# Sliding-window attention with a gated SwiGLU branch on one core: scores in sixteen 32x32 tiles, first loads in smaller pieces

## The chip, the core and the metric

The kernel runs on one core of a Trainium2 chip. A core has TensorE (PE, matrix multiplies, with its weight loads shown apart as PEld), VectorE (DVE), ScalarE (ACT), GpSimd (POOL) and SyncE (SP, which here only issues DMAs). The metric is the device time of one execution in microseconds; smaller is better.

## The reference

For one sequence of 2048 tokens of width 512, the output mixes two branches by a gate per token. Branch a is attention with 32 heads of 16 dimensions, where a query sees its own token and the 255 before it; branch b is a SwiGLU feed-forward network of inner width 1376.

```python
g = sigmoid((x * gate_w).sum(-1, keepdims=True))
qkv = (x @ wqkv).reshape(B, S, 3, H, Dh)          # H = 32, Dh = 16, W = 256
scores = einsum("bhqd,bhkd->bhqk", q, k) * Dh ** -0.5
mask = (i_q - i_k >= 0) & (i_q - i_k < W)
p = softmax(where(mask, scores, -1e9))
a = einsum("bhqk,bhkd->bhqd", p, v).reshape(B, S, D) @ wo
b = (silu(x @ w1) * (x @ w3)) @ w2
return g * a + (1 - g) * b
```

## The kernel before

Everything is in bf16 with f32 sums. The sequence is cut into four chunks t of 512 tokens, and the 32 heads into four groups c of eight heads (128 rows of Q and K).

**Attention.** `add_proj` (line 294) projects K and Q of a group and a chunk. K is written twice, with the even heads' rows zeroed in one copy and the odd heads' in the other (`maskEO`), so that 32 rows hold two heads and 128 columns hold 64 keys for the even head and the same 64 keys for the odd one. A score step, called a burst (`add_burst`, line 664), takes two or three pieces: each is a block of 64 keys with the queries of this chunk that can see any of them, up to 320. `bursts` (line 272) lists the pieces; their columns add up to 512 at most. For each piece four matmuls with 32 rows and 128 columns of weights (line 685) write the scores of eight heads, transposed, into four PSUM banks called `big`. There is one `big`, so a burst waits until the previous burst's exp has read it. ACT takes the exp of the whole of it (line 693) into an `e` tile; triangles at the near and far end of each piece are then zeroed by POOL (affine_select, line 709) or DVE (a minimum with `keep`, line 703). There are 76 bursts, 19 for each group. The product with V (`add_pv`, line 730; matmuls at line 759) takes the `e` tiles of a chunk in eight tiles of 64 rows and 32 columns, with a column of ones in V for the denominators; DVE transposes, divides and transposes back into `OT`.

**Feed-forward, gate and output.** `add_up` (line 442) makes gate and up products and their swish, `add_up_last` the last 96 inner rows in tiles of 128x32 (line 505), `add_down` (line 543) the second product; `add_out` (line 574) multiplies by `wo`, mixes and stores, in two DMAs a row block for m under 8 and in one for the rest. `add_last` does the last row block.

**Order.** The kernel plans itself: each piece of work is an `Op` with engines, a duration and what it waits for; a list scheduler (lines 873 to 1003) places them by these costs, and the instructions are then issued in that order, engine by engine. Bursts have due times, `T0 + PACE * n`. Once placed, an engine's order is fixed, and the chip's engines meet through semaphores alone.

**Start.** TensorE runs six warm-up matmuls on a zeroed tile (line 1008). Meanwhile the first loads are issued: SP issues x0 and x1 (256 tokens each), q0 (both of the first two groups' Q weights), k1, v, and then transposing loads and feed-forward weights; ACT issues k0. The first 512 tokens are transposed by TensorE (`add_tx`, line 230), which needs the identity `ident` from POOL, and copied to `xT` by DVE and ACT; later tokens come through transposing DMAs.

Of the kernel before, what the change touches and what calls it, by code (L numbers as in the profile page):

```python
# [8 lines left out]
ACT = mybir.ActivationFunctionType  # L9
# [5 lines left out]
WIN = 256  # L15
P = 128
# [6 lines left out]
def kernel(  # L23
# [77 lines left out]
    def slot(pool, key):  # L101
        return slot_of[(pool, key)]

    warm = sb.tile([P, 1, P], BF16, name="tt0")
    nc.vector.memset(warm[:], 0.0)
    nc.vector.memset(scr[:], 0.0)  # L106
    xs_tiles = {}

    def x_dma(t, h):
        xs = xp.tile([P, 2, D], BF16, name=f"xs{h}")[:]  # L110
        nc.sync.dma_start(
            out=xs,
            in_=x2d[512 * t + 256 * h:512 * t + 256 * (h + 1), :].rearrange("(m p) d -> p m d", p=P))
        xs_tiles[2 * t + h] = xs

    def xt_dma(t, c):
        nc.sync.dma_start_transpose(out=xT[:, c, 512 * t:512 * (t + 1)],
# [13 lines left out]
        land[name] = at  # L131

    nc.scalar.activation(out=scr[:, 1:2], in_=scr[:, 0:1], func=ACT.Tanh)
    dma("x0", "SP", 3.8, lambda: x_dma(0, 0))
    dma("x1", "SP", 4.8, lambda: x_dma(0, 1))
    dma("k0", "ACT", 4.6, lambda: w_dma(nc.scalar, wk_sb, A_wqkv, 0, P, D))
    dma("q0", "SP", 6.2, lambda: w_dma(nc.sync, wq_sb, A_wqkv, 0, 2 * P))
    dma("k1", "SP", 7.0, lambda: w_dma(nc.sync, wk_sb, A_wqkv, P, 2 * P, D))
    dma("v", "SP", 8.5, lambda: w_dma(nc.sync, wv_sb, A_wqkv, 0, D, 2 * D))
    dma("x2", "SP", 11.2, lambda: [xt_dma(1, c) for c in range(NDC)])  # L140
    FA = 4 * P
    dma("wa", "SP", 14.4, lambda: (w_dma(nc.sync, w1_sb, B_w1, 0, FA),
# [87 lines left out]
    def add_tx(m2):  # L230

        xT_op[m2] = []
        for half in range(2):
            key = ("tx", m2, half)
            hold("g", key, 1)
            cs = slice(2 * half, 2 * half + 2)

            def pe(key=key, half=half):
                tx = bank(key, BF16, (P, 2, 2, P))
                for j in range(2):  # L240
                    for c in range(2):
                        d0 = (2 * half + c) * P
                        nc.tensor.transpose(out=tx[:, j, c, :], in_=xs_tiles[m2][:, j, d0:d0 + P],
                                            identity=ident[:])

            def evac(eng, key=key, cs=cs):
                dst = xT[:, cs, 2 * m2 * P:(2 * m2 + 2) * P].rearrange("p c (j t) -> p j c t", j=2)
                if eng == "ACT":
                    nc.scalar.copy(out=dst, in_=g_tile[key][:])
                else:  # L250
                    nc.vector.tensor_copy(out=dst, in_=g_tile[key][:])

            a = Op("PE", 0.25 if m2 > 1 else 0.43, pe, [loads[f"x{m2}"]], acq=[("g", key)], kind="tx")
            a.first, a.need = m2 < 2, 9.0
            xT_op[m2].append(Op("ACT" if half else "DVE", 0.55 if half else 0.36, evac, [a],
                                rel=[("g", key)], rank=-1))

    def xdep(t0, t1):

        r = []  # L260
        for c in range(NDC):
            r.append([xT_op[m2][c // 2] if m2 < 2 else loads["x2" if m2 < 4 else "x4" if m2 < 6 else "x6"]
                      for m2 in range(t0 // 256, (t1 + 255) // 256)])
        return r

    LAST = (NDC - 1, NTC - 1)
# [27 lines left out]
    def add_proj(c, t0, t1, is_q):  # L294


        key = ("q" if is_q else "k", c, t0)
        t = t0 // 512
        hold("g", key, 1)
        n = t1 - t0  # L300
        o0 = t0 - 512 * t
        first = (c, t, "alloc") not in qk_tile
        if first:
            hold("qk", (c, t), len(bursts(c, t)) + (len(bursts(c, t + 1)) if t + 1 < NTC else 0))

        def pe(d0):
            def fn():
                if (c, t) not in qk_tile:
                    i = slot("qk", (c, t))
                    qk_tile[(c, t)] = (sb.tile([P, 1024], BF16, name=f"kt{i}"),  # L310
                                       sb.tile([P, 512], BF16, name=f"qt{i}"))
                b = bank(key) if d0 == 0 else g_tile[key]
                for dc in range(d0, d0 + 1):
                    nc.tensor.matmul(b[:, 0:n], lhsT=(wq_sb if is_q else wk_sb)[:, dc, c * P:(c + 1) * P],  # L314
                                     rhs=xT[:, dc, t0:t1], start=(dc == 0), stop=(dc == NDC - 1))
            return fn

        def evac_q(eng):
            qt = qk_tile[(c, t)][1]
            if eng == "ACT":  # L320
                nc.scalar.copy(out=qt[:, o0:o0 + n], in_=g_tile[key][:, 0:n])
            else:
                nc.vector.tensor_copy(out=qt[:, o0:o0 + n], in_=g_tile[key][:, 0:n])

        def evac_k(eng):
            kt = qk_tile[(c, t)][0][:, 2 * o0:2 * (o0 + n)].rearrange("p (j i b) -> p j i b", i=2, b=HK)
            src = g_tile[key][:, 0:n].rearrange("p (j x b) -> p j x b", x=1, b=HK)
            sh = [P, n // HK, 2, HK]
            nc.vector.tensor_tensor(out=kt, in0=src.to_broadcast(sh), in1=maskEO[:].to_broadcast(sh),
                                    op=ALU.mult)  # L330

        w = loads[("q0" if is_q else f"k{c}") if c <= 1 else "kq"]
        a0, a = pe_unit(0.216 * NDC * n / 512, [pe(i) for i in range(NDC)],
                        [w] + ([] if first else [qk_tile[(c, t, "alloc")]]),
                        acq=[("g", key)] + ([("qk", (c, t))] if first else []), kind="proj",
                        more=xdep(t0, t1))
        if first:
            qk_tile[(c, t, "alloc")] = a0
        d = 0.68 * n / 512 + 0.03
        if is_q:  # L340
            bs = [Op(("ACT", "DVE"), d, evac_q, [a], rel=[("g", key)], rank=-0.5)]
            Q_op.setdefault(c, []).append((t0, t1, bs))
        else:
            bs = [Op("DVE", 1.16 * n / 512 + 0.05, evac_k, [a], rel=[("g", key)], rank=-0.5)]
            K_op.setdefault(c, []).append((t0, t1, bs))
        return a0
# [227 lines left out]
    def add_out(m, n0=0, n1=512):  # L574
# [13 lines left out]
        def fin(eng):  # L588
            ot = smpool.tile([P, D], BF16, name="ot")
            nc.vector.scalar_tensor_tensor(out=ot[:, 0:n], in0=g_tile[key][:, 0:n],  # L590
                                           scalar=gq[:, m:m + 1], in1=bsb[:, m, n0:n1],
                                           op0=ALU.mult, op1=ALU.add)
            for i in range(0, n, n // (2 if m < 8 else 1)):
                j = i + n // (2 if m < 8 else 1)
                nc.sync.dma_start(out=out2d[m * P:(m + 1) * P, n0 + i:n0 + j], in_=ot[:, i:j])

        a0, a = pe_unit(0.87 * n / 512, [pe(i) for i in range(NDC)], [pv_out[(c, m)] for c in range(NDC)] + [loads["wo"], down_pe[m]],
# [66 lines left out]
    def add_burst(c, t, n):  # L664


        key = (c, t, n)
        pieces = bursts(c, t)[n]
        w = sum(q1 - q0 for _, q0, q1, _ in pieces)
# [3 lines left out]
        for j, q0, q1, _ in pieces:  # L673
            deps += cover(K_op, c, HK * j, HK * j + HK) + cover(Q_op, c, q0, q1)
        deps = list(dict.fromkeys(deps))
        tl = {}

        def pe():
            qt = qk_tile[(c, t)][1]
            big = ps.tile([P, 4, 512], F32, name="big")  # L680
            tl["big"] = big
            for j, q0, q1, col in pieces:
                kt = qk_tile[(c, j // 8)][0]
                for u in range(4):
                    nc.tensor.matmul(big[:, u, col:col + q1 - q0],  # L685
                                     lhsT=kt[32 * u:32 * u + 32, (j % 8) * P:(j % 8 + 1) * P],
                                     rhs=qt[32 * u:32 * u + 32, q0 - 512 * t:q1 - 512 * t],
                                     start=True, stop=True)

        def ex(eng):  # L690
            e = sb.tile([P, 4, 512], BF16, name=f"e{slot('e', key)}")
            e_tile[key] = e
            nc.scalar.activation(out=e[:, :, 0:w], in_=tl["big"][:, :, 0:w], func=ACT.Exp,  # L693
                                 scale=SCALE)

        def mask(cols, far):
            def f(eng):
# [14 lines left out]
                                                channel_multiplier=1 if far else -1)  # L712
            return f

        a = Op("PE", 0.21 + 0.22 * w / 512, pe, deps, acq=[("big", key)], kind="burst",
               rel=[("qk", (c, t))] + ([("qk", (c, t - 1))] if t else []))
        b = Op("ACT", 0.13 + 1.75 * w / 512, ex, [a], rel=[("big", key)], acq=[("e", key)],
               rank=-1, kind="exp")
# [82 lines left out]
            pv_out[(c, m)] = o  # L801
        return a

    T0, PACE, NWARM = 11.5, 2.59, 6
    SEQ = [(t, n) for t in range(NTC) for n in range(len(bursts(0, t)))]
    per_c = len(SEQ)

# [13 lines left out]
    for c in range(NDC):  # L821
        pieces = [(0, 256), (256, 512)] if c == 0 else [(0, 512)]
        pieces += [(512 * t, 512 * t + 512) for t in range(1, NTC)]
        for t0, t1 in pieces:
            for is_q in ((True, False) if (c, t0) == (1, 0) else (False, True)):
                a = add_proj(c, t0, t1, is_q)
                lead = (4.0 if is_q or t0 else 5.0) if c == 0 else 6.0 + (4 - t0 / 512) * 4.0
                a.need = when(c, first_use(c, t0, t1, is_q)) - lead
# [176 lines left out]
    with tc.manual_schedule():  # L1005
        b = ps.tile([P, 512], F32, name="g0")
        for i in range(NWARM):
            nc.tensor.matmul(b[:], lhsT=warm[:, 0, :], rhs=warm[:].to_broadcast([P, 4, P]), start=(i == 0),  # L1008
                             stop=(i == NWARM - 1))
        done = set()  # L1010
        for o in order:
            if not wo_t and o in burst_ops[7:] and done.issuperset(z_op[0:4]):
# [34 lines left out]
```

The softmax here doesn't subtract the row's maximum and nothing guards it: scores larger than these inputs give would overflow.

## Time and profile before

| what | value |
|---|---|
| median of 3 runs | 231.02 us (231.02 to 231.4) |
| the profiled execution | 230.87 us |
| its span, first to last instruction | 229.2 us |
| granted TensorE clock over the span | 1.0 |
| weight loads and matmuls | 3060 each |
| matmuls of the bursts (line 685) | 720 in 76 bursts |
| matmuls of the V product (line 759) | 1440 in 16 runs |
| x0 / x1 landed | 3.93 / 5.02 us |

"Busy" of an engine is the time in which at least one of its instructions ran. Matmuls are pipelined: a record runs from the start of a matmul to its modelled end, which comes well after the next one has started, so starts are what to compare. "Idle before" is the time in which an engine ran nothing before a group, with what ended it.

### The profile page before, as it was taken

How to read it: one execution, taken by the hardware profiler on the slowest of the kernel's cores; microseconds unless marked ns; L12 is line 12 of the kernel's file. 1: busy time of each engine (PE TensorE's matmuls, PEld its weight loads, DVE VectorE, ACT ScalarE, POOL GpSimd, SP SyncE). 2: the span in 40 equal slices, each digit the busy share in tenths (PEclk: the TensorE clock that was granted, in tenths of full speed). 3: DMA queues.
4: the chain of work that ended last, by engine and by line, in shares of the span. 5: the costliest groups of instructions: out<-in, count | busy, mean ns of one | idle time of the engine just before them, and what ended most of it. 6: DMA issues, size and time to landing. Idle time of an engine off the chain costs nothing.

```text
span 229.2 us, 7274 instructions
## 1 busy us (share of the span) xinstructions
PE 224.8 (98%) x3060; PEld 101.2 (44%) x3060; DVE 180.9 (79%) x316; ACT 175.5 (77%) x144; POOL 174.7 (76%) x395
## 2 busy tenths in 40 slices
PE   7999999999999999999999999999999999999995
PEld 3544434544344443544353435444443444354544
DVE  1688599999998997879758596959987688876754
ACT  3578889788989989787989897987899877977030
POOL 8058888888899898888878887877888878777200
PEclk9999999999999999999999999999999999999999
DMA  6999999401000000000000000000000001220202
GB/s 186 235 255 301 234 268 338 112 0 27 26 3 3 3 0 0 3 4 4 0 3 0 3 3 3 0 3 4 0 3 1 3 4 37 70 82 0 94 3 93
DMA packets 20081, 13.81 MB, mean 60 GB/s; under 512 B 8656, under 2 KB 19760, under 8 KB 20048
## 3 DMA queue, kind: packets, MB, share of 16 engines
q1 hardware_dynamic: 18944, 11.93, 18.8%
q0 software_dynamic: 432, 1.25, 2.8%
q8 instruction: 24, 0.39, 0.7%
q10 hardware_dynamic: 672, 0.16, 0.3%
q14 instruction: 9, 0.07, 0.1%
HBM read 8.55 MB, written 2.10 MB: 46 GB/s over the span
## 4 chain that ended last, share of the span: by engine, by line
PE 97%; DMA 2%; SPq 0%; DVE 0%; issue 0%
PE big L685 11%; DMA xs_93<-in_A_x_dram 2%; PE g_1928 L553 1%; PE g_2556 L553 1%; PE g_3349 L553 1%; PE g_2293 L553 1%; PE g_3614 L553 1%; PE g_4324 L553 1%; PE g_4389 L553 1%; PE g_3016 L553 1%; PE g_3813 L553 1%; PE g_2755 L553 1%; PE g_1650 L553 1%; PE g_1297 L553 1%; PE g_4284 L553 1%; PE g_2168 L553 1%
## 5 line engine op out<-in xcount | busy, mean ns | idle before, releaser
L455 PEld LDWEIGHTS <-w_sb 128*128 128x128 bf16 x320 | 29.2, 98 | 35.3 <-issue 3.4
L759 PEld LDWEIGHTS <-Vn 64*32 64x32 bf16 x720 | 15.1, 91 | 2.9 <-issue 1.3
L759 PEld LDWEIGHTS <-Vs 64*32 64x32 bf16 x720 | 15.2, 91 | 0.2
L784 DVE STREAM_TRANSPOSE OT<-on 128x512 bf16<-128x512 bf16 x16 | 11.3, 703 | 0.1
L314 PEld LDWEIGHTS <-wk_sb 128*128 128x128 bf16 x68 | 6.0, 98 | 7.2 <-issue 1.5
L361 PEld LDWEIGHTS <-xT 128*128 128x128 bf16 x64 | 5.7, 98 | 7.4 <-issue 1.6
L314 PEld LDWEIGHTS <-wq_sb 128*128 128x128 bf16 x68 | 6.0, 98 | 6.4 <-issue 1.5
L583 PEld LDWEIGHTS <-OT 128*128 128x128 bf16 x60 | 5.6, 97 | 6.8 <-issue 0.2
L709 POOL TENSOR_SCALAR_AFFINE_SELECT e_246<-e_246 64x256 bf16<-64x256 bf16 x6 | 2.5, 411 | 7.8 <-ACT e_246 L693 7.5
L553 PEld LDWEIGHTS <-hT_680 128*128 128x128 bf16 (+1 forms) x44 | 4.0, 98 | 5.1 <-issue 0.8
L553 PEld LDWEIGHTS <-hT_2291 128*128 128x128 bf16 (+1 forms) x44 | 4.0, 98 | 5.0 <-issue 0.6
L397 DVE SCALAR_TENSOR_TENSOR OT<-OT 128x512 bf16<-128x512 bf16 x8 | 5.9, 760 | 0.0
L553 PEld LDWEIGHTS <-hT_345 128*128 128x128 bf16 (+1 forms) x44 | 3.9, 98 | 4.3
L559 ACT ACTIVATE bsb<-g_4389,omg 128x512 bf16<-128x512 f32 x1 | 0.7, 687 | 6.2 <-PE g_4389 L553 6.2
L553 PEld LDWEIGHTS <-hT_3272 128*128 128x128 bf16 (+1 forms) x33 | 3.1, 97 | 3.8 <-issue 0.2
L709 POOL TENSOR_SCALAR_AFFINE_SELECT e_1530<-e_1530 64x256 bf16<-64x256 bf16 x6 | 3.7, 611 | 0.3
L709 POOL TENSOR_SCALAR_AFFINE_SELECT e_1261<-e_1261 64x256 bf16<-64x256 bf16 x6 | 3.6, 596 | 0.3
L1008 PE MATMUL g_144<-tt_86 128*128 128x512 bf16 x6 | 2.7, 630 | 1.1 <-DVE scr L106 1.1
L709 POOL TENSOR_SCALAR_AFFINE_SELECT e_976<-e_976 64x256 bf16<-64x256 bf16 x6 | 3.2, 528 | 0.6 <-ACT e_976 L693 0.3
L709 POOL TENSOR_SCALAR_AFFINE_SELECT e_3832<-e_3832 64x256 bf16<-64x256 bf16 x6 | 2.5, 411 | 1.1 <-ACT e_3832 L693 0.8
L709 POOL TENSOR_SCALAR_AFFINE_SELECT e_2774<-e_2774 64x256 bf16<-64x256 bf16 x6 | 2.5, 411 | 1.1 <-ACT e_2774 L693 0.8
L709 POOL TENSOR_SCALAR_AFFINE_SELECT e_1787<-e_1787 64x256 bf16<-64x256 bf16 x6 | 3.1, 512 | 0.3
(929 smaller groups left out, 852.5 us busy)
## 6 DMA issues: line engine op xcount, KB each, us to landing
w_sb<-in_B_w_dram SPq DMA_DIRECT2D x2, 864.0 KB, 8.0
w_sb<-in_B_w_dram SPq DMA_DIRECT2D x1, 1280.0 KB, 8.6
Vs<-Vn POOLq DMA_DIRECT2D x8, 136.0 KB, 3.9
out_dram<-ot SPq DMA_DIRECT2D x17, 64.0 KB, 1.6
w_sb<-in_B_w_dram SPq DMA_DIRECT2D x2, 512.0 KB, 4.7
OT<-in_A_x_dram SPq DMA_DIRECT2D x1, 1024.0 KB, 10.8
out_dram<-ot SPq DMA_DIRECT2D x7, 128.0 KB, 2.2
wq_sb<-in_A_wqkv_dram SPq DMA_DIRECT2D x2, 256.0 KB, 6.2
```

Source lines behind the costliest of these rows:

```text
L314: nc.tensor.matmul(b[:, 0:n], lhsT=(wq_sb if is_q else wk_sb)[:, dc, c * P:(c + 1) * P], rhs=xT[:, dc, t0:t1], start=(dc == 0), stop=(dc = ...
L361: nc.tensor.matmul(b[:], lhsT=xT[:, c, m * P:(m + 1) * P], rhs=wv_sb[:, c, :], start=(c == 0), stop=(c == NDC - 1))
L397: nc.vector.scalar_tensor_tensor(out=x, in0=x, scalar=1.0, in1=gw, op0=ALU.mult, op1=ALU.mult, accum_out=zt[:, m:m + 1])
L455: nc.tensor.matmul(b[:], lhsT=wsb[:, dc, f * P:(f + 1) * P], rhs=xT[:, dc, t * 512:(t + 1) * 512], start=(dc == 0), stop=(dc == NDC - 1))
L553: nc.tensor.matmul(b[:], lhsT=h_tile[t][0:fs, f, (m % 4) * P:(m % 4 + 1) * P], rhs=w2_sb[0:fs, f, :], start=(f == 0), stop=(f == NFC - 1))
L559: nc.scalar.activation(out=bsb[:, m, :], in_=g_tile[key][:], func=ACT.Copy, scale=omg[:, m:m + 1])
L583: nc.tensor.matmul(b[:, 0:n], lhsT=OT[:, c * S + m * P:c * S + (m + 1) * P], rhs=wo_t[c // 2][:, c % 2, n0:n1], start=(c == 0), stop=(c == ...
L685: nc.tensor.matmul(big[:, u, col:col + q1 - q0], lhsT=kt[32 * u:32 * u + 32, (j % 8) * P:(j % 8 + 1) * P], rhs=qt[32 * u:32 * u + 32, q0 - ...
L709: nc.gpsimd.affine_select(out=tri, in_=tri, pattern=[[0, 4], [-1 if far else 1, HK]], compare_op=ALU.is_ge, fill=0.0, base=-1 if far else ...
L759: nc.tensor.matmul(pv[i][32 * u:32 * u + 32, a - qa:b - qa], lhsT=v_of(j, i, 4 * c + u), rhs=e_tile[k][i * HK:i * HK + HK, u, col:col + b ...
L784: nc.vector.transpose(out=OT[:, c * S + qa:c * S + qb], in_=st["on"][:, 0:nb].rearrange("p b i d -> p (b i d)"))
L1008: nc.tensor.matmul(b[:], lhsT=warm[:, 0, :], rhs=warm[:].to_broadcast([P, 4, P]), start=(i == 0), stop=(i == NWARM - 1))
```

## The change

The score matmuls are cut from 32x128 tiles into 32x32 ones. Each of the four 32-column quarters v of a key block (two quarters of keys for the even head, two for the odd one) is now a matmul of its own, so a piece is sixteen matmuls instead of four. The later 32 keys of a block leave out the first 32 queries of the near end, the earlier 32 keys leave out the last 32 queries of the far end: those scores are all masked. What is left out in PSUM is what stood there before; it is masked after the exp, as before. `big` becomes one tile for the whole kernel and is zeroed once by DVE.

The first 256 tokens of x are loaded by two DMAs of 128 tokens, one from SP and one from ACT, and transposed and copied row block by row block. The load q0 is split into q0 and q1. The warm-up multiplies a constant of ones, which needs no memset. The planned landing times, the cost of a burst (less the cut columns), T0 and the order of the first Q and K projections follow; output row blocks 6 and 7 are stored in one DMA each.

```diff
-    warm = sb.tile([P, 1, P], BF16, name="tt0")
-    nc.vector.memset(warm[:], 0.0)
     nc.vector.memset(scr[:], 0.0)
+    big = ps.tile([P, 4, 512], F32, name="big")
+    nc.vector.memset(big[:], 0.0)
...
+    def x_dma1(j):
+        if j == 0:
+            xs_tiles[0] = xp.tile([P, 2, D], BF16, name="xs0")[:]
+        (nc.scalar if j else nc.sync).dma_start(out=xs_tiles[0][:, j, :], in_=x2d[j * P:(j + 1) * P, :])
...
-    dma("x0", "SP", 3.8, lambda: x_dma(0, 0))
-    dma("x1", "SP", 4.8, lambda: x_dma(0, 1))
-    dma("k0", "ACT", 4.6, lambda: w_dma(nc.scalar, wk_sb, A_wqkv, 0, P, D))
-    dma("q0", "SP", 6.2, lambda: w_dma(nc.sync, wq_sb, A_wqkv, 0, 2 * P))
-    dma("k1", "SP", 7.0, lambda: w_dma(nc.sync, wk_sb, A_wqkv, P, 2 * P, D))
-    dma("v", "SP", 8.5, lambda: w_dma(nc.sync, wv_sb, A_wqkv, 0, D, 2 * D))
+    dma("x00", "SP", 3.5, lambda: x_dma1(0))
+    dma("x01", "SP", 3.6, lambda: x_dma1(1))
+    dma("x1", "SP", 4.5, lambda: x_dma(0, 1))
+    dma("k0", "ACT", 4.8, lambda: w_dma(nc.scalar, wk_sb, A_wqkv, 0, P, D))
+    dma("q0", "SP", 5.8, lambda: w_dma(nc.sync, wq_sb, A_wqkv, 0, P))
+    dma("k1", "SP", 6.3, lambda: w_dma(nc.sync, wk_sb, A_wqkv, P, 2 * P, D))
+    dma("q1", "SP", 6.8, lambda: w_dma(nc.sync, wq_sb, A_wqkv, P, 2 * P))
+    dma("v", "SP", 8.2, lambda: w_dma(nc.sync, wv_sb, A_wqkv, 0, D, 2 * D))
...
+            def pe_row(key=key, half=half):
+                tx = bank(key, BF16, (P, NDC, P))
+                for c in range(NDC):
+                    nc.tensor.transpose(out=tx[:, c, :], in_=xs_tiles[0][:, half, c * P:(c + 1) * P],
+                                        identity=ident[:])
...
-            for i in range(0, n, n // (2 if m < 8 else 1)):
-                j = i + n // (2 if m < 8 else 1)
+            for i in range(0, n, n // (2 if m < 6 else 1)):
+                j = i + n // (2 if m < 6 else 1)
...
             qt = qk_tile[(c, t)][1]
-            big = ps.tile([P, 4, 512], F32, name="big")
-            tl["big"] = big
             for j, q0, q1, col in pieces:
                 kt = qk_tile[(c, j // 8)][0]
-                for u in range(4):
-                    nc.tensor.matmul(big[:, u, col:col + q1 - q0],
-                                     lhsT=kt[32 * u:32 * u + 32, (j % 8) * P:(j % 8 + 1) * P],
-                                     rhs=qt[32 * u:32 * u + 32, q0 - 512 * t:q1 - 512 * t],
-                                     start=True, stop=True)
+                k0 = (j % 8) * P
+                for v in range(4):
+                    a = q0 + (32 if v % 2 and q0 == HK * j else 0)
+                    b = q1 - (32 if v % 2 == 0 and q1 == HK * j + WIN + HK else 0)
+                    for u in range(4):
+                        nc.tensor.matmul(big[32 * v:32 * v + 32, u, col + a - q0:col + b - q0],
+                                         lhsT=kt[32 * u:32 * u + 32, k0 + 32 * v:k0 + 32 * v + 32],
+                                         rhs=qt[32 * u:32 * u + 32, a - 512 * t:b - 512 * t],
+                                         start=True, stop=True, skip_group_check=True)
...
-        a = Op("PE", 0.21 + 0.22 * w / 512, pe, deps, acq=[("big", key)], kind="burst",
+        cut = 16 * sum((q0 == HK * j) + (q1 == HK * j + WIN + HK) for j, q0, q1, _ in pieces)
+        a = Op("PE", 0.21 + 0.22 * (w - cut) / 512, pe, deps, acq=[("big", key)], kind="burst",
...
-    T0, PACE, NWARM = 11.5, 2.59, 6
+    T0, PACE, NWARM = 11, 2.59, 6
...
-            for is_q in ((True, False) if (c, t0) == (1, 0) else (False, True)):
+            for is_q in (False, True):
...
-            nc.tensor.matmul(b[:], lhsT=warm[:, 0, :], rhs=warm[:].to_broadcast([P, 4, P]), start=(i == 0),
-                             stop=(i == NWARM - 1))
+            nc.tensor.matmul(b[:], lhsT=nc.const_aps.tensor(1.0, (P, P), BF16),
+                             rhs=nc.const_aps.tensor(1.0, (P, 512), BF16), start=(i == 0), stop=(i == NWARM - 1))
```

## The prediction

> **What bounds the kernel now.** I read the page's busy part first, then its chain, then the waits of TensorE, then the group of the score matmuls by their line, and last the timeline around single bursts.
>
> ```profile
> PE 224.8 (98%) x3060; PEld 101.2 (44%) x3060; DVE 180.9 (79%) x316; ACT 175.5 (77%) x144; POOL 174.7 (76%) x395
> PE 97%; DMA 2%; SPq 0%; DVE 0%; issue 0%
> ...
> PE g_144 L1008 <- DVE scr L106: 1.1, 1, 1.1
> PE g_162 L243 <- DMA xs_93<-in_A_x_dram: 0.4, 1, 0.4
> PE g_151 L243 <- DMA xs_91<-in_A_x_dram: 0.2, 1, 0.2
> ```
>
> The last three lines are all that TensorE waited for, and all lie before 5.1 us. From there to its end it is never starved, and DVE, ACT and POOL keep a fifth of their time free. So the time is the moment at which TensorE starts for good, plus the sum of its work, plus a tail of about 2 us. A change is priced by what TensorE gains or loses.
>
> ```profile
>   issue: 32.2, 76
> ...
> 40.20 0.38 PE L455 MATMUL g_740<-xT,w_sb 128*128 128x512 bf16 x1
> 40.51 0.37 PE L685 MATMUL big<-qt_603,kt_602 32*128 32x320 bf16 x8
> 40.71 0.20 PE L685 MATMUL big<-qt_603,kt_252 32*128 32x64 bf16 x4
> 40.84 0.32 PE L759 MATMUL g_759<-e_388,Vn 64*32 64x320 bf16 x4
> ...
> 41.29 0.31 PE L759 MATMUL g_759<-e_530,Vn 64*32 64x320 bf16 x4
> ```
>
> A burst (four heads of one score step, line 685) is 8 or 12 matmuls, four of which stream side by side: 512 columns in all are 0.213 us at the 216 ns that a 512-column matmul takes here. Around it stand about 0.10 us before the first (40.20 + 0.216 = 40.416, and it starts at 40.51) and 0.09 us after the last stream (40.71 + 0.027 for 64 columns = 40.74, and the next mode starts at 40.84). With some 0.02 us of stagger a burst costs 0.43 us of TensorE; 76 of them are 33 us.
>
> The change makes each burst 32 or 48 small matmuls. The place in the trace where small ones stand densely is the PV product (line 759, 96 matmuls in eight tiles of 64x32). I counted its loads (PEld) and matmuls (PE) up to a growing end, from just before its start at 40.84:
>
> ```profile
> core 0: us, PE busy (x) PEld busy (x), PEclk, DMA share, GB/s
> 40.83:40.90 0.07, 0.06 (x8) 0.06 (x16) 1.00 0.64 219
> 40.83:41.54 0.71, 0.70 (x64) 0.66 (x65) 1.00 0.40 137
> 40.83:41.60 0.77, 0.76 (x64) 0.72 (x65) 1.00 0.38 130
> 40.83:41.62 0.79, 0.78 (x64) 0.74 (x66) 1.00 0.37 127
> 40.83:41.70 0.87, 0.86 (x72) 0.82 (x76) 1.00 0.34 118
> ```
>
> Three things are read here. First, at the start loads and matmuls come quickly: the first eight matmuls lie within 0.025 us in the timeline, some 3.3 ns a pair. Second, the 65th load is out by 41.54 and the 66th only at 41.62, though its tile's earlier weights were in use from 41.51. The 33rd matmul (the first on e_530) starts at 41.29 and its record ends at about 41.59; the 66th load follows about 0.03 us later. So some 33 pairs can be open, and a place comes free when a matmul ends, not when it starts. Third, from 41.62 to 41.70 ten loads go out: about 8.3 ns a pair once the stock is used up.
>
> **What the skill says.** The Trainium skill, "TensorE: Matmul & The Clock Gate", Terms and the table at its top, gives TensorE a queue of 64 entries with a partial reorder window for weight loads; 33 pairs of load and matmul agree with that. Its Part 3 prices sixteen 32x32 tiles as the length of one matmul plus about 4 ns for each further tile; the 3.3 ns above agree, but that price is for one set of sixteen, and no run shown so far has sixteen. "TensorEngine Tiling (Array Packing)", Key Properties, says that a change of tiling mode drains the engine: the 0.09 to 0.10 us on both sides of a burst agree, and 64x32 pays the same as 32x128, so I take the same for 32x32. "DMA: Bandwidth & Descriptors", Issuing engines are not separate DMA queues, says that a second issuing queue saves the issue time alone; here one issue takes 0.44 to 0.47 us.
>
> **The change, part by part.**
>
> Score tiles, two-piece bursts. The built order has 76 bursts as before, 48 of two pieces (32 pairs) and 28 of three (48 pairs). Thirty-two pairs fit the window. The sixteenth matmul of a piece starts 15 x 3.3 = 50 ns after the first, where the fourth started 10 ns after it: 40 ns later at the end. Against it stand shorter streams: the two cuts take 32 columns from each tile's 320, 13 ns, and a second piece gives its last tile another 0 or 13. Followed by tile, the last stream of the types 320+192 ends 12 ns or 25 ns later than now, of 256+256 25 ns, of 320+64 11 ns. Per group of heads that is 35 ns for the first chunk and 62 for each of three others, 0.22 us; times four, +0.9 us. Bounds: 0 (the stagger closes up) and +2.
>
> Score tiles, three-piece bursts. The first piece's matmuls start over 50 ns; one of 288 columns ends in the records after 288/2.4 = 120 ns plus some 170 ns (a 64x320 one shows 0.31 us, of which 0.133 are stream), so at 0.29 us. Until then 32 or 33 pairs are open and the third piece cannot be loaded. Its loads begin at 0.29 + 0.03 = 0.32 and follow at 8.3 ns: the last at about 0.32 + 15 x 8.3 ns = 0.45. Its 32 or 64 columns stream to 0.475, where the burst now ends at 0.24. That is +0.235 us; times 28, **+6.6 us**. Bounds: +0.8 in all if places come free at a matmul's start (only the stagger, 29 ns each), +8 if the refill comes 0.05 later.
>
> What is queued behind: the next full-size matmul needs two entries and the drain, and has both. PV bursts behind a score burst find a thinner stock; they are limited by their streams (about 90 ns for eight pairs, 66 at the refill rate), so +0.1 for all 16 (0 to 0.5). The built order has one mode change more (178 for 177), +0.1. The exp starts after the burst's last matmul, later by the same amount, and the next burst comes later by as much too; its slack stays.
>
> One big tile for all bursts, and its memset. Four PSUM banks as before, one burst at a time as before: a burst waits for ACT's exp in both. The memset writes 2048 f32 on DVE; DVE's 512-element PSUM rows take 0.68 us, so up to 2.7 us, from 0.95 to at most 3.7. DVE's next operation waited until 4.20 for POOL's eo: hidden. If it ran past that, the first xT copy (4.49) would follow late, by tenths.
>
> First loads. Now x0 lands at 3.93 and x1 at 5.02; TensorE is continuous from 5.06. Transposes can't start before POOL has made ident (3.34 + 0.29 = 3.63), so an earlier x0 brings little. The x1 load is issued at 1.31 as before, but k0 (128 KB) stands behind x01 on ACT's queue and competes with less of it: at the 350 GB/s of the records between 4 and 5 us half of 128 KB is 0.2 us. k0 itself lands about 0.5 later than its 4.27, still before the K projection needs it at about 5.3. Half a q0 is enough for the first Q; k1 and q1 come before their use at about 7 and 8. SP issues one DMA more ahead of v, so v and everything behind it (transposing loads, w1, w3) start up to 0.5 us later. w1's first part landed at 13.05 for a use at 15.06, and v at 7.91 for a use at 9.01: covered. Sum: -0.2 us (bounds -0.6 and +0.3).
>
> Warm-up on a constant: it starts at about 0.9 instead of 1.06, ends earlier, and TensorE then waits for ident and x0 as before. Cost and gain nothing; the cover is that wait. T0, the Q/K order and the halved DMAs up to m 5 instead of 7 move work within a full TensorE: nothing, since those outputs leave long before the end.
>
> Sum: +0.9 + 6.6 + 0.1 + 0.1 - 0.2 = +7.5 us. The profiled execution took 230.87 (its span 229.2 and 1.7 around it), 0.15 under the median of 231.02. 230.87 + 7.5 = 238.4.
>
> **The rivals.** (A) The window holds back third pieces: 238.4, chance 0.65, own range 236.5 to 241. For it speaks the 66th load. Against it: no burst of sixteen tiles is in the trace.
>
> (B) The window does not bind with tiles of this size, only the stagger costs: 28 x 29 ns = 0.8, +0.9, +0.2, -0.2 = +1.7: 232.6, chance 0.14.
>
> (C) Faster: the later pieces close the stagger up, so only the shorter streams count. They are 800 columns per group of heads (128 in the first chunk, 224 in each other), 3200 in all, 1.3 us; with 0.5 at the start -1.8: 229.1, chance 0.13. It decides from where a three-piece burst's last matmul starts under 0.2 us after its first. Against it: in PV the eight tiles keep their 3.3 ns stagger from piece to piece.
>
> (D) Worse: the stock is not full at a burst's start because TensorE's sequencer stands at the wait for the exp. At 8.3 ns for every pair, two-piece bursts then end 0.11 later too, 48 x 0.11 = +5: 243, chance 0.08. Against it: the exps end 0.2 us or more before nearly all bursts, time for some 24 pairs.
>
> **How the numbers follow.** The time is A's. The range 231.3 to 241.5 takes in A, nearly all of B and the lower edge of D. A measurement of this kernel tells 0.2% (0.5 us) from no change: faster 0.13 (C), same 0.03 (between B and C), slower 0.84.
>
> **What would show it.** Right: three-piece bursts occupying about 0.66 us from the preceding stream to the next, two-piece ones about 0.45; TensorE still without waits after 5 us; start at about 4.9. Wrong: three-piece bursts at or under 0.45 (B, C), two-piece ones above 0.5 (D), or a new wait of TensorE at its start, on k0 above all.

## The result, and the profile after

The changed kernel takes 247.25 us (median of 6 runs, 246.55 to 248.72), where the kernel before takes 231.01 (230.9 to 231.4 beside it on the same chip): a ratio of 1.0707, 95% interval 1.0676 to 1.0737. The forecast was 238.4 with a range up to 241.5. The direction was right, and less than half of the added time was foreseen. The profiled execution of after took 246.55 us, with a span of 244.8 against 229.2 and a clock of 0.998: 15.6 us of span have to be found.

The page of after, parts 1, 3 and 4 (busy time and instructions; the DMA queue that carries instructions, with packets, MB and share; the chain by engine):

```profile
PE 234.9 (96%) x5220; PEld 111.6 (46%) x5220; DVE 184.8 (75%) x315; ACT 175.9 (72%) x145; POOL 172.0 (70%) x395
...
q8 instruction: 41, 0.67, 1.2%
...
PE 91%; DMA 4%; issue 2%; SPq 1%; DVE 0%; DVEq 0%
```

The same line of part 3 in the page of before:

```profile
q8 instruction: 24, 0.39, 0.7%
```

TensorE is still the engine of the chain, but its share fell from 97% to 91%: there are now holes in it. And a queue that the prediction does not mention grew: q8, 24 packets of 16 KB before and 41 after. TensorE has 3060 loads and as many matmuls before, 6120, and 10440 after; divided by 256 that is 23.9 and 40.8. So q8 carries TensorE's own instructions, 256 in a packet (a block, below). The waits of TensorE in after (what waited for what; us in total, times, longest) say where the holes are:

```profile
PE big L715 <- issue: 4.0, 6, 1.1
...
PE g_1085 L790 <- issue: 0.5, 1, 0.5
PE g_216 L388 <- DMA e_89<-in_A_wqkv_dram: 0.3, 1, 0.3
```

"Issue" is time in which the engine waited for nothing that the profile shows: no semaphore, no buffer. The view counts from the modelled end of the last matmul, and so shows only part of each hole. The kernel before had no wait of this kind. The timeline of TensorE in after, around one of them (start, length, instructions):

```profile
30.31 0.39 PE L532 MATMUL g_744<-xT,w_sb 128*32 128x512 bf16 x4
30.63 0.33 PE L715 MATMUL big<-qt_278,kt_277 32*32 32x288 bf16 x12
31.90 0.30 PE L715 MATMUL big<-qt_278,kt_277 32*32 32x288 bf16 x4 [0.94 <-issue]
31.91 0.25 PE L715 MATMUL big<-qt_278,kt_176 32*32 32x96 bf16 x12
```

Twelve of the first piece's sixteen matmuls start at 30.63, and the other four 1.27 us later, in the middle of a burst whose inputs and bank are all there. The DMA view of the stretch from 29.50 to 29.70 holds the last packet of q8 before that:

```profile
q8 instruction: 1, 0.02, 29.2%
```

It starts at 29.58, and work resumes at 31.90, 2.3 us later.

There are ten such gaps of 0.25 to 1.34 us from one start to the next (at 30.67, 37.71, 44.48, 48.93, 60.18, 77.14, 88.34, 113.88, 166.62 and 204.13), and a small one of 0.14 at 141.26. What a gap costs is read here, and in all runs below, as what its burst or product takes beyond the median of the same kind (for full-size matmuls, beyond the 0.216 us of a stream): the eleven cost 6.6 us together. Counting all matmuls and loads from the start up to each gap (windows; the (x) behind PE and PEld are counts) gives a pattern:

```profile
core 0: us, PE busy (x) PEld busy (x) DVE busy (x) ACT busy (x) POOL busy (x), PEclk, DMA share, GB/s
0.00:31.50 31.50, 29.68 (x478) 14.17 (x478) 21.03 (x39) 21.10 (x23) 20.73 (x54) 1.00 1.07 223
0.00:38.30 38.30, 35.73 (x606) 16.51 (x606) 26.76 (x48) 25.93 (x27) 26.07 (x66) 1.00 1.07 241
0.00:114.30 114.30, 109.68 (x2396) 51.58 (x2397) 91.36 (x168) 84.38 (x75) 86.41 (x195) 1.00 0.43 101
0.00:205.30 205.30, 199.43 (x4572) 93.60 (x4573) 159.75 (x275) 157.33 (x131) 154.72 (x356) 1.00 0.25 59
```

478 + 478 = 956 = 3 x 256 + 188. 606 + 606 = 1212 = 4 x 256 + 188. 2396 + 2397 = 4793 = 18 x 256 + 185. 4572 + 4573 = 9145 = 35 x 256 + 185. All eleven counts leave 185 to 188: TensorE stops at the same place of a block of 256 instructions.

The bursts themselves look as forecast. The timeline of a three-piece burst in after, and the windows of its line's instructions alone from its start:

```profile
13.80 0.38 PE L341 MATMUL g_279<-xT,wk_sb 128*128 128x512 bf16 x1
14.11 0.64 PE L715 MATMUL big<-qt_177,kt_176 32*32 32x288 bf16 x48
14.68 0.39 PE L341 MATMUL g_336<-xT,wq_sb 128*128 128x512 bf16 x1
```

```profile
core 0: us, PE busy (x) PEld busy (x), PEclk, DMA share, GB/s
14.10:14.14 0.04, 0.03 (x9) 0.03 (x10) 1.00 1.08 384
14.10:14.28 0.18, 0.17 (x27) 0.17 (x33) 1.00 1.08 380
14.10:14.35 0.25, 0.24 (x32) 0.23 (x33) 1.00 1.07 374
14.10:14.42 0.32, 0.31 (x32) 0.23 (x33) 1.00 1.10 373
14.10:14.50 0.40, 0.39 (x41) 0.29 (x41) 1.00 1.11 368
14.10:14.60 0.50, 0.49 (x48) 0.40 (x48) 1.00 1.10 348
```

Nine matmuls start in the first 0.03 us. The 33rd load is out by 14.28, and no other follows until after 14.42, over 0.3 us after the burst's start. That is the window of 33 open pairs. From the end of the preceding stream (13.80 + 0.216) to the next start (14.68) are 0.66 us.

The account of the span, from the two traces:

| where | us |
|---|---|
| 28 three-piece bursts, 0.666 us for 0.430 | +6.6 |
| 48 two-piece bursts, 0.452 us for 0.428 | +1.15 |
| eleven gaps in TensorE's supply | +6.6 |
| start: first burst at 11.51 for 11.48, with one matmul (0.216) fewer ahead of it | +0.25 |
| tail: start of the last matmul to the end, 4.1 for 3.0 | +1.1 |
| sum (span: 15.6) | +15.7 |

The tail is read from the chain of after at its end (start, length, what):

```profile
237.74 0.76 DVE ot L617
...
238.52 3.44 DMA out_dram<-ot
...
242.08 0.35 DVE ot L670
```

The last piece of output (line 670) waits until a store, issued at 238.52, has emptied one of the four `ot` buffers: 3.44 us, where the median of the page for the stores on that queue is 1.7 (128 KB) and 2.2 (64 KB). In before the chain ends with matmuls and the last piece of output, and no store holds it up.

### The profile page after: what moved, and what is told of

Read it like the earlier page. It is cut to its first block, busy times and chain, and to the rows that moved or that the text cites. A ratio compares the mean times of both kernels' runs of the same rounds, so it can differ in the third digit from the quotient of the medians.

```text
span 244.8 us, 11599 instructions
## 1 busy us (share of the span) xinstructions
PE 234.9 (96%) x5220; PEld 111.6 (46%) x5220; DVE 184.8 (75%) x315; ACT 175.9 (72%) x145; POOL 172.0 (70%) x395
## 4 chain that ended last, share of the span: by engine, by line
PE 91%; DMA 4%; issue 2%; SPq 1%; DVE 0%; DVEq 0%
PE big L715 14%; DMA e_89<-in_A_wqkv_dram 2%; DMA out_dram<-ot 1%; PE g_2620 L580 1%; PE g_2357 L580 1%; PE g_1877 L580 1%; PE g_6308 L580 1%; PE g_4026 L580 1%; PE g_2965 L580 1%; PE g_5277 L580 1%; PE g_3699 L580 1%; PE g_6383 L580 1%; PE g_3322 L580 1%; PE g_6473 L580 1%; PE g_4897 L580 1%
## 5 line engine op out<-in xcount | busy, mean ns | idle before, releaser
L739 POOL TENSOR_SCALAR_AFFINE_SELECT e_269<-e_269 64x256 bf16<-64x256 bf16 x6 | 2.9, 490 | 7.9 <-ACT e_269 L723 7.7
L739 POOL TENSOR_SCALAR_AFFINE_SELECT e_1809<-e_1809 64x256 bf16<-64x256 bf16 x6 | 3.7, 613 | 1.1 <-ACT e_1809 L723 0.8
L739 POOL TENSOR_SCALAR_AFFINE_SELECT e_954<-e_954 64x256 bf16<-64x256 bf16 x6 | 2.5, 410 | 2.2 <-ACT e_954 L723 1.9
L715 PEld LDWEIGHTS <-kt_277 32*32 32x32 bf16 x192 | 1.9, 88 | 4.4 <-issue 4.2
L715 PEld LDWEIGHTS <-kt_4826 32*32 32x32 bf16 x192 | 1.9, 88 | 3.6 <-issue 3.4
L723 ACT ACTIVATE e_5891<-big 128x2048 bf16<-128x2048 f32 x1 | 1.9, 1877 | 2.3 <-PE big L715 2.3
L1039 PE MATMUL g_146<-const-bfloat16-1.0 128*128 128x512 bf16 x6 | 2.7, 626 | 0.8 <-PEq L1062 0.8
L739 POOL TENSOR_SCALAR_AFFINE_SELECT e_1264<-e_1264 64x256 bf16<-64x256 bf16 x4 | 2.6, 643 | 1.2 <-ACT e_1264 L723 1.0
```

The source lines that it names most:

```text
L715: nc.tensor.matmul(big[32 * v:32 * v + 32, u, col + a - q0:col + b - q0], lhsT=kt[32 * u:32 * u + 32, k0 + 32 * v:k0 + 32 * v + 32], rhs=q ...
L723: nc.scalar.activation(out=e[:, :, 0:w], in_=big[:, :, 0:w], func=ACT.Exp, scale=SCALE)
L739: nc.gpsimd.affine_select(out=tri, in_=tri, pattern=[[0, 4], [-1 if far else 1, HK]], compare_op=ALU.is_ge, fill=0.0, base=-1 if far else ...
L1039: nc.tensor.matmul(b[:], lhsT=nc.const_aps.tensor(1.0, (P, P), BF16), rhs=nc.const_aps.tensor(1.0, (P, 512), BF16), start=(i == 0), stop=( ...
```

## The experiments

The theory after the result is one of supply: TensorE's instructions come in blocks of 256, a block takes some 3 us to come, and where a block is used up faster TensorE stands. There are three rivals: the changed first loads and planned order cost the rest; 32x32 tiles themselves stall now and then; or the gaps belong to certain places of the program, such as a buffer or a bank that is not shown.

**Loads and order alone, tiles alone.** The first run puts the four 32x128 matmuls back into the changed kernel; the second puts the sixteen tiles into the kernel before.

```diff
-                for v in range(4):
...
+                for u in range(4):
+                    nc.tensor.matmul(big[:, u, col:col + q1 - q0],
+                                     lhsT=kt[32 * u:32 * u + 32, k0:k0 + P],
```

> The changed kernel with the score matmuls put back to four tiles of 32x128 (720 matmuls again); loads, warm-up, planner constants and order stay those of the changed kernel. Theory (window of open pairs plus instruction supply, both caused by the 2160 added matmuls): nearly the whole loss goes; no stall of TensorE without a releaser, 24 instruction refills, bursts 0.43 us each; 231.0 to 231.6. Rival (the new first loads cost time, by v landing late[...]): 232.5 or more, with v landing near 9.2 us.

> The kernel before, its loads and its order, with only the score matmuls in sixteen 32x32 tiles. Theory: window +6.5 and stagger +1.0 as predicted, plus 5 to 7 us of stalls at one place in every 256 TensorE instructions, which lie elsewhere than in the changed kernel since the order differs: 243 to 246. Rival (the prediction's own sum, stalls being an effect of the new order or of the loads): 238.5, without stalls.

Loads and order alone: 231.39 us, ratio 1.0008 (0.9996 to 1.0021), no difference that can be told; bursts 0.43 us, 24 packets on q8, one gap of 0.2 us (in a product with V, at a count of 955), and the first burst at 10.78. The tiles alone: 245.44 us, ratio 1.0631 (1.0604 to 1.0658), 41 packets, nine gaps of 4.7 us, bursts 0.451 and 0.666, tail 4.3, and the first burst 0.7 later than in before (12.22). The tiles carry the loss, and the rival of the loads and the order falls. The gaps stand at counts of the same kind (957, 1213, 3002 and so on); but seven of the nine lie in the same bursts, by number, as gaps of after, so that this run doesn't tell a place in the block from a place in the program.

**Two-piece or three-piece bursts alone.** The other kind keeps its four matmuls; for the second run the line reads `== 2`.

```diff
+                if len(pieces) == 3:
...
+                    for u in range(4):
+                        nc.tensor.matmul(big[:, u, col:col + q1 - q0],
...
+                    continue
```

> The changed kernel with sixteen tiles in the 48 two-piece bursts only; the 28 three-piece bursts are back in four tiles. Theory: two-piece bursts 0.44 to 0.45 us, three-piece ones 0.43, so no window cost, +1.0 for the stagger, and 0 to 2 us of stalls, since a stretch of 256 instructions takes longer when the three-piece burst next to a V product is short: 232 to 234. Rival (loss in proportion to the added matmuls, 1152 of 2160): 231 + 0.53 x 16 = 239.5.

> The changed kernel with sixteen tiles in the 28 three-piece bursts only. Theory: three-piece bursts 0.66 us, two-piece ones 0.43: +6.5, and 2 to 5 us of stalls: 239.5 to 242.5. Rival (loss in proportion to the added matmuls, 1008 of 2160): 231 + 0.47 x 16 = 238.5.

Two-piece bursts in sixteen: 232.58 us, ratio 1.0049 (1.003 to 1.0069). They cost 0.451 us, the others 0.430. There is no gap of this kind, though q8 moves nine blocks more than before; TensorE waits once, 0.9 us longer than usual at 43.3, for DVE, which itself had waited for a load:

```profile
q8 instruction: 33, 0.54, 1.0%
```

Three-piece bursts in sixteen: 241.64 us, ratio 1.0462 (1.0432 to 1.0492), bursts of 0.665, five gaps of 2.2 us, tail 4.6. So the two halves, +1.5 and +10.6 us, don't add up to the whole of +16.2, and neither do the gaps, 0 and 2.2 for 6.6. A cost that each small matmul bears would add up; a supply that is enough up to a rate and not beyond does not.

**The same number of instructions in the old tiles; half as many small ones.** The first keeps four 32x128 tiles and cuts each matmul into four of a quarter of the columns, 2880 in all as in after. The second uses 32x64 tiles, 1440 matmuls, without the cut columns.

```diff
+                n4 = (q1 - q0) // 4
                 for v in range(4):
...
+                   for u in range(4):
+                     nc.tensor.matmul(big[:, u, col + v * n4:col + v * n4 + n4],
+                                      lhsT=kt[32 * u:32 * u + 32, k0:k0 + P],
```

> The changed kernel with the old four tiles of 32x128 for the scores, but each of those matmuls split along its queries into four of a quarter of the width: again 2880 score matmuls, no tile of 32x32, no cut columns. Theory (the number of TensorE instructions is what costs): 41 instruction refills, stalls at the same place in every 256 instructions, 4 to 7 us of them; three-piece bursts 0.55 to 0.60 us, since the pairs from the 33rd on again wait for the first matmuls to end, which are short here; two-piece ones 0.44 to 0.47. In all 239 to 243. Rival (sixteen 32x32 tiles are slow by themselves): bursts 0.43 us, no stalls, 231 to 232.

> The changed kernel with eight tiles of 32x64 for the scores (all keys of one head in a tile, no cut): 1440 score matmuls, 16 or 24 pairs in a burst, which is under the 33 that can be open. Theory: both kinds of burst 0.44 to 0.46 us, no jump for three pieces; 29 or 30 refills with hardly a stall (0 to 1 us): 232 to 234. Rival (a fixed price for each added matmul, 0.235 us for 36 of them in the three-piece bursts): +0.08 for 12, +0.05 for 8, so 235.5 or more.

Quarter widths in the old tiles: 244.75 us, ratio 1.0594 (1.0533 to 1.0655), above the 239 to 243 expected, because of ten gaps of 7.7 us instead of 4 to 7 and a tail of 4.0. Their counts, 956, 1212, 1467, 1723, 2234, 3001, 3513, 4793, 6073 and 9145, are all counts of gaps in after too. The rival of the tile's form falls: with the same number of instructions the gaps come in tiles of the old form as well. The burst, in the timeline:

```profile
13.79 0.38 PE L341 MATMUL g<-xT,wk_sb 128*128 128x512 bf16 x1
14.11 0.54 PE L714 MATMUL big<-qt,kt 32*128 32x80 bf16 x48
14.58 0.61 PE L341 MATMUL g<-xT,wq_sb 128*128 128x512 bf16 x2
```

From 13.79 + 0.216 to 14.58 are 0.574 us, 0.09 less than with 32x32 tiles. This is the window again: a matmul of 80 columns has 208 columns less to stream than one of 288, 88 ns at 0.216 us for 512, so the first places come free that much earlier.

32x64 tiles: 233.39 us, ratio 1.0087 (1.0064 to 1.011), one gap of 0.5 us, at a count of 4793, and 29 packets for 7560 instructions. A three-piece burst has 24 pairs here:

```profile
13.05 0.59 PE L341 MATMUL g<-xT,wk_sb 128*128 128x512 bf16 x2
13.57 0.43 PE L715 MATMUL big<-qt,kt 32*64 32x320 bf16 x24
13.93 0.82 PE L341 MATMUL g<-xT,wq_sb 128*128 128x512 bf16 x3
```

Bursts of both kinds take 0.453 to 0.455 us. With 16 and with 24 pairs it is the same, with 32 still 0.452, with 48 it is 0.666: the jump lies between 32 and 48, where the window of 33 puts it.

**The same program, its instructions moved along.** The warm-up is 48 matmuls of 64 columns instead of six of 512, so all later instructions stand 84 further on in TensorE's stream.

```diff
-        for i in range(NWARM):
+        for i in range(48):
...
-                             rhs=nc.const_aps.tensor(1.0, (P, 512), BF16), start=(i == 0), stop=(i == NWARM - 1))
+                             rhs=nc.const_aps.tensor(1.0, (P, 64), BF16), start=(i == 0), stop=(i == 47))
```

> The changed kernel with the six 512-column warm-up matmuls replaced by 48 of 64 columns: the same warm-up time, and 84 TensorE instructions more ahead of all the rest. Theory: the stalls keep their place in every 256 instructions, counted from the first one (about 185 to 190 modulo 256), and so fall on other bursts than in the changed kernel; 4 to 9 us of stalls in all, 244 to 250. Rival (the stalls belong to certain bursts, for what those wait for): the same bursts stall as in the changed kernel, at an instruction count that is 84 higher modulo 256.

It takes 245.68 us, ratio 1.0619 (1.0582 to 1.0656), with nine gaps of 6.8 us. TensorE in the timeline around the first, and the counts up to the first three:

```profile
28.71 0.31 PE L790 MATMUL g<-e,Vn 64*32 64x320 bf16 x3
30.54 0.31 PE L790 MATMUL g<-e,Vn 64*32 64x320 bf16 x1 [1.51 <-issue]
```

```profile
core 0: us, PE busy (x) PEld busy (x) DVE busy (x) ACT busy (x) POOL busy (x), PEclk, DMA share, GB/s
0.00:30.40 30.40, 27.85 (x478) 15.25 (x478) 18.91 (x35) 20.58 (x22) 20.31 (x53) 1.00 1.14 229
0.00:37.10 37.10, 32.98 (x606) 17.37 (x606) 24.07 (x43) 23.53 (x25) 24.25 (x61) 1.00 1.10 239
0.00:48.80 48.80, 43.78 (x861) 22.39 (x862) 34.47 (x62) 32.64 (x32) 31.96 (x79) 1.00 1.01 227
```

The counts are 956, 1212 and 1723 = 6 x 256 + 187, so the same place in the block; in the program the first gap moved out of a burst into a product with V, two microseconds earlier. All nine counts leave 185 to 188, and none of the five bursts with a gap has one in after. The rival of a place in the program falls: the gaps stay with the count and leave the piece of work.

**One output buffer more.** `ot` gets five buffers instead of four.

```diff
-    smpool = ctx.enter_context(tc.tile_pool(name="sm", bufs=4))
+    smpool = ctx.enter_context(tc.tile_pool(name="sm", bufs=5))
```

> The changed kernel with five output buffers instead of four. Theory for its longer tail (the last output tile waits for a buffer whose store lands late, next to the last instruction refill): the last VectorE operation follows TensorE's last matmul at once, the tail from the last matmul to the end is 3 us instead of 4, and the time is 246.2, 1.0 below the changed kernel's median; hard to tell from its spread of 2 us by times alone, so the profile decides. Rival (the tail is long for another reason): tail still 4 us.

The chain at its end has no store any more, and the tail is 3.02 us:

```profile
238.40 2.45 PE g L664 x33
240.85 0.03 issue
240.88 0.35 DVE ot L670
```

So the buffer is what the last output waited for. The whole takes 245.05 us (244.42 to 245.77), a ratio to before of 1.0591 (1.0552 to 1.0629); 2.2 us under the median of after. The tail accounts for 1.1 of it. The two profiled executions differ by 1.2 us (246.55 and 245.35), almost the tail alone; the rest of the medians' difference is within the 2.2 us over which the times of after spread.

**Looking for a version that beats before.** Without the tiles the first burst starts 0.7 us earlier than in before, and yet the time is equal. In its profiled execution 0.2 us of that is a matmul of 512 columns that now stands behind the burst, 0.2 goes into the one gap and 0.1 into the tail. Two runs gave the changed kernel with four tiles other due times, T0 = 11.75 and 11.25 instead of 11.

```diff
-    T0, PACE, NWARM = 11, 2.59, 6
+    T0, PACE, NWARM = 11.75, 2.59, 6
```

> Four score tiles with the new first loads and warm-up, and T0 = 11.75 in place of 11, which gives TensorE an order with 174 changes of tiling mode (177 before, 178 in the changed kernel). Theory: the start is 0.3 to 0.5 us earlier, as in the kernel with the loads alone, and three drains of 0.1 us less than before are saved; no late instruction refill: 230.2 to 230.6, against 231.1 for the kernel before. Rival (the start's gain is given back later whatever the order): 231.0 to 231.4.

> The same with T0 = 11.25: 175 changes of tiling mode. Theory: 230.3 to 230.7. Rival: 231.0 to 231.4.

Both missed: 232.17 us (ratio 1.0043, 1.0028 to 1.0058) and 231.7 (1.0027, 1.0016 to 1.0039). TensorE's waits with 11.75 show what other orders bring:

```profile
PE g L482 <- DVE kt L356: 0.4, 2, 0.2
...
PE g L787 <- POOL e L736: 0.2, 1, 0.2
```

These are real waits on DVE's K copies and POOL's triangles, which neither before nor the run with T0 = 11 has. (This trace lacks 33 of the 3060 matmul records; most of the short waits for "issue" that the view lists beside these stand where a record is missing.) No version here is faster than before.

## Why the prediction was wrong

**What bounds the kernel.** Held. TensorE's work and waits make the time, and none of the loss lies elsewhere except in the tail.

**Three-piece bursts.** Right in mechanism and size: +0.235 us was forecast for each and +0.236 measured, 6.6 in all. The 33 open pairs, the end of a matmul as what frees a place, and the refill were read from the product with V, and they held for another tile; two runs (80 columns, 24 pairs) confirm it from two sides. Rival B, that the window would not bind, and C, that the burst would close up, both fall with 0.666 us.

**Two-piece bursts.** +0.9 forecast, +1.15 measured. The stagger is there; D, which wanted 0.11 us for each, falls with 0.024.

**What is queued behind, and the sum: the step that failed.** It asked what the added instructions do in the array and in the queue ahead of it, and took for granted that they are there. "The next full-size matmul needs two entries and the drain, and has both", it said of what follows a burst, and the sum ends without a term for the supply. The change adds 4320 instructions of TensorE to 6120 in the same time, and they are not spread evenly. Twenty-eight bursts have 96 each within 0.66 us, and a product with V, unchanged, has 192 in some 1.2 us: one behind the other, 288 instructions in about 1.8 us. In a quiet part of after a block that TensorE had to wait for took 3.3 us, from the passing of the place at 111.17 to the resumption at 114.48; at the other such places after 50 us, where the bulk loads are over, 3.1 to 3.8 us, and 4.15 at the last. Seven blocks were used up there in 2.7 to 3.2 us, from one place to the next, and TensorE stood after each; all others lasted 3.7 us or more, and it stood after none. In before the quickest block lasted about 4.9 us (188.34 to 193.21), so nothing ran out, although 256 instructions in a row that lie across two blocks took as little as 2.8 (from 150.57). The missing term is 6.6 us, most of the miss of 8.85 between 238.4 and 247.25. The lines that would have pointed to it stood in before: 24 packets on an instruction queue in part 3 of its page, and 192 instructions in a row in the product with V. How long a block takes they could not show, since nothing stood there.

The Trainium skill has a passage on this: "Runtime: NRT & Kernel Launch", Instruction fetch mechanics. It says that an engine's instructions come in blocks of 16 KiB, 256 instructions, over a DMA queue of the sequencer's own, and that this is mostly hidden. The 256 agree with 24 and 41 packets here. That it is hidden holds for before and for the sixteen-tile two-piece bursts (33 packets, no gap), not for after. The section gives TensorE room for 2048 instructions, eight blocks, and also says that the store of instructions is only two blocks. The measurements fit a lead of about one block: a block that lasts under some 3 us is enough to make TensorE stand, though the blocks before it lasted longer. No run here varied the lead.

**Products with V.** +0.1 forecast. They take 0.9 us more in all, of which 0.7 is one gap of the supply (at 44.48); without it the forecast holds.

**First loads.** -0.2 forecast, about +0.25 measured: wrong in sign, inside its bounds. K started 0.2 earlier (5.33 for 5.52), as meant, and not more, because the four sets of transposes follow each other at 0.37 to 0.47 us where the last two of before take 0.23 (why is open: the granted clock in the records is 1.00, and they follow at 0.46 us with the tiles and the old loads, at 0.3 with the new loads and the old tiles). Then v landed at 9.20 instead of 7.91, so that TensorE waited 0.3 us for it at its first V projection. "v at 7.91 for a use at 9.01: covered" was the error: the cover was 1.1 us and the delay 1.3. In other runs with the same loads v landed at 7.65 to 9.2 us (8.10 with the four tiles), so this term is uncertain by about what it is worth. The memset of `big` (1.36 to 3.12 us) stayed hidden, as forecast.

**The tail.** "A tail of about 2 us" was taken as fixed, and "those outputs leave long before the end". From the start of the last matmul to the end it was 3.0 us in before, and it is 1.1 us longer in after because a store holds its buffer for longer. The run of tiles alone, which keeps the two stores for row blocks 6 and 7, has the longer tail too, so the merged stores aren't its cause.

**What stays open.** When exactly the fetch of a block is asked for. Ahead of the gaps of after in quiet times the packet starts 0.7 to 1.8 us after the place in the block is passed, while bulk loads run up to 4 us (passed at 31.90, packet at 35.85), and work resumes 2.3 to 2.9 us after the packet starts; that the loads delay it is argued from these times, and no run tried it. Where nothing stands, some packets start before the place is passed (186.54 for 188.34 in before). Why the store in the tail took 3.44 us is open too. A packet of q8 started 0.9 us after it, at 239.42. In the five runs in which a packet falls 0.9 to 1.8 us behind such a store it took 3.4 to 3.9 us; in the run with the instructions moved along, whose last packet came at 232.22, the same store took 1.70 and the tail 3.0. That speaks for the packet as the cause, but it rests on one execution of each run, and how a packet would hold up a store isn't shown.

## What to carry to other kernels

Before cutting matmuls into more and smaller ones, count instructions as well as array time: how long each block of 256 instructions lasts, against the 3.1 to 4.2 us that the next one took here in quiet times, and how many load and matmul pairs stand in a row, against the 33 that can be open. Bursts of up to 32 pairs cost almost nothing extra here, and 48 pairs cost half as much again. An idle "issue" in the middle of a burst, at counts that leave nearly the same remainder when divided by 256, was the mark of a supply that had run out here.

## What was not expected of the hardware

TensorE's supply of instructions can be the limit: 256 in 3.3 us in quiet times is one instruction in 13 ns, or a load and its matmul in 26, where TensorE took such a pair in 3.3 ns from its stock and in 8.3 ns once the stock was used up. The limit is not additive: 33 blocks in 231 us made no gap and 41 in 245 made gaps of 6.6 us, because only dense stretches count. And the gaps move with the stream: 84 instructions of warm-up shifted them to other work and left their sum about the same (6.8 us for 6.6), so that a small edit far ahead can move the time of an unchanged part: the first product with V, which had no gap in after, took 1.8 us longer.
